# Reordering the first loads of a two-layer attention and gated-MLP kernel, with twelve idle matmuls ahead of them

## The chip, the cores and the metric

The kernel runs on one core of a Trainium2 chip. The metric is the time of one execution in device microseconds (us), from 1 core; several executions are timed and the median is quoted. A profile records one execution. Its span, from the first to the last instruction, is 1.8 us shorter than the time of the same execution (span 1628.9 belongs to 1630.68). Ratios are computed as the mean time of one kernel's runs over that of the other's of the same rounds, so they are not quite the ratio of the medians that are quoted.

## The reference, cut to what matters

```
x = x + A(layernorm(x))      # linear attention, D = 1024, 32 heads, S = 2048 rows
x = x + B(layernorm(x))      # gated MLP, F = 3584
x = x + A(layernorm(x))      # the same weights again
x = x + B(layernorm(x))
```

Only the beginning of the first A matters: normalise rows of x, transpose them, and multiply by the weights of k (`wqkv[:, D:2D]`). Weights and x are bf16, sums f32.

## The kernel before

S is worked on in blocks of 128 rows: x0, x1 and so on are such blocks (256 KB each in bf16). Weights come in tiles of 1 MB (`k0`, `k1`: the two halves of the k weights, 8 slices of 128 rows by 512 columns). The first four blocks go through a hand-ordered head:

```python
def head(self):
    H = self.KT // 2                        # 4: half of the 8 slices of a weight tile
    zero = self.ep.tile([P, NW], BF16, tag="e")
    nc.vector.memset(zero, 0.0)
    idle = self.ps3.tile([P, NW], F32, tag="b")
    for _ in range(10):                     # nothing uses them: they only keep PE working
        nc.tensor.matmul(idle, lhsT=zero[:, 0:P], rhs=zero, start=True, stop=True)

    k0, k1, v0, q0, q1 = (ring.place() for _ in range(5))
    self.load_x(0, 0, nc.scalar)            # first half of x0 on ACT's queue
    self.load_x(0, 1)                       # second half on SP's queue
    self.load_x(1, None, nc.scalar)
    k0(0, H)                                # weights are on SP's queue
    self.load_x(2, None, nc.scalar)
    k0(H, 2 * H)
    self.load_x(3, None, nc.scalar)
    k1()
    q0()
    self.load_x(4)
    ...                                     # x5 and later, q1, v0
```

```python
def block0():                               # head_units: order of DVE and ACT is as written
    stat(0, 0)                              # DVE: statistics of x0, first half
    stat(0, 1)
    rstd(0)                                 # DVE, then two ACTIVATEs
    stat(1, 0)                              # DVE: fills the wait for rstd, needs x1
    scale(0, 0)                             # DVE
    scale(0, 1)
    t0 = turn(0, 0)                         # PE: four transposes
    t1 = turn(0, 1)
    t0("s")                                 # ACT copies them to SBUF
    stat(1, 1)
    rstd(1)
    t1("v")                                 # DVE copies
    k(0, 0, between)                        # PE: 8 matmuls, x0 with k0; `between` turns x1
```

The fifth matmul of `k(0, 0)` is the first to need the second half of k0. The next eight are x1 with k0, the eight after that x0 with k1, and only then come the transposes of x2.

Of the kernel before, what the change touches and what calls it, by code (L numbers as in the profile page):

```python
# [18 lines left out]
class _Ring:  # L19
# [9 lines left out]
    def place(self):  # L29

        name, src = self.plan[self.loaded]
        t = self.pool.tile([P, 8, NW], BF16, tag="w")
        self.tiles[name] = t
        self.loaded += 1
        return lambda lo=0, hi=8: self.nc.sync.dma_start(out=t[:, lo:hi, :], in_=src[:, lo:hi, :])

    def load_to(self, n):
        while self.loaded < min(n, len(self.plan)):
# [40 lines left out]
class _Net:  # L79
# [131 lines left out]
    def head(self):  # L211

        nc, tc, ring = self.nc, self.tc, self.ring
        H = self.KT // 2

        zero = self.ep.tile([P, NW], BF16, tag="e")
        nc.vector.memset(zero, 0.0)
        idle = self.ps3.tile([P, NW], F32, tag="b")
        for _ in range(10):
            nc.tensor.matmul(idle, lhsT=zero[:, 0:P], rhs=zero, start=True, stop=True)  # L220

        k0, k1, v0, q0, q1 = (ring.place() for _ in range(5))
        self.load_x(0, 0, nc.scalar)
        self.load_x(0, 1)
        self.load_x(1, None, nc.scalar)
        k0(0, H)
        self.load_x(2, None, nc.scalar)
        k0(H, 2 * H)
        self.load_x(3, None, nc.scalar)
        k1()  # L230
        q0()
        self.load_x(4)
        self.load_x(5)
        self.load_x(6)
        self.load_x(7)
        q1()
        for t in range(8, self.ST):
            self.load_x(t)
        v0()
        src = self.xb  # L240
        self.xnT[0, 0] = self.xnTp.tile([P, self.KT, QT * P], BF16, tag="xnT", name="xnT0_0")
        stats = [self.small.tile([P, 2, nc.vector.BN_STATS_DIM], F32, tag="stats", name=f"st{j}")
                 for j in range(QT)]
        rs, xn = {}, {}

        def stat(j, c):
            self.ln_stat(j, src[j], c, stats[j])

        def rstd(j):
            rs[j] = self.ln_rstd(stats[j])  # L250
            xn[j] = self.xn_home(0, j)

        def scale(j, h=None):
            self.ln_scale(src[j], *rs[j], xn[j], h)

        def turn(j, h):
            tp = self.ps3.tile([P, H, P], BF16, tag="b")
            for i in range(H):
                kt = h * H + i
                nc.tensor.transpose(tp[:, i, :], xn[j][:, kt * P:(kt + 1) * P], self.ident)  # L260
            dst = self.xnT[0, 0][:, h * H:(h + 1) * H, j * P:(j + 1) * P]

            def take(engine):
                if engine == "v":
                    nc.vector.tensor_copy(out=dst, in_=tp)
                else:
                    nc.scalar.activation(out=dst, in_=tp, func=ACT.Copy)

            return take

        return stat, rstd, scale, turn
# [468 lines left out]
```

## Time and profile before

| | before |
|---|---|
| median time | 1629.3 us (1629.17 to 1629.80, 4 runs) |
| profiled execution | 1630.68 us, span 1628.9 us |
| PE busy | 1621.7 us of the span |
| wait of PE for the second half of k0 | 1.73 us |
| its load: issued, landed | 1.66, 10.19 us |

The list of DMA issues for the moment at which the second half of k0 (SP) and x2 (ACT) are issued; the columns are what is loaded, the issuing queue, count, size, and us from issue to landing:

```profile
t<-in_A_wqkv_dram SPq DMA_DIRECT2D x1, 512.0 KB, 8.5
x<-in_A_x_dram ACTq DMA_DIRECT2D x1, 256.0 KB, 7.7
```

Both are issued within 0.01 us and both take about 8 us, and x3 follows on ACT's queue: the three are moved at the same time.

### The profile page before, as it was taken

How to read it: one execution, taken by the hardware profiler on the slowest of the kernel's cores; microseconds unless marked ns; L12 is line 12 of the kernel's file. 1: busy time of each engine (PE TensorE's matmuls, PEld its weight loads, DVE VectorE, ACT ScalarE, POOL GpSimd, SP SyncE). 2: the span in 40 equal slices, each digit the busy share in tenths (PEclk: the TensorE clock that was granted, in tenths of full speed). 3: DMA queues.
4: the chain of work that ended last, by engine and by line, in shares of the span. 5: the costliest groups of instructions: out<-in, count | busy, mean ns of one | idle time of the engine just before them, and what ended most of it. 6: DMA issues, size and time to landing. Idle time of an engine off the chain costs nothing.

```text
span 1628.9 us, 18772 instructions
## 1 busy us (share of the span) xinstructions
PE 1621.7 (100%) x7754; PEld 739.3 (45%) x7754; DVE 566.7 (35%) x940; ACT 331.8 (20%) x638; POOL 201.9 (12%) x134
## 2 busy tenths in 40 slices
PE   8999999999999999999999999999999999999999
PEld 4444444444444444444444444444444444444444
DVE  7845695213212222212165547942022111111211
ACT  5741212101110110111066312121011101101110
POOL 2349220000000000000023592100000000000000
DMA  7312647448445444544560147464554454454452
GB/s 245 65 52 56 178 71 206 144 148 232 155 143 190 160 151 161 168 147 137 168 128 1 53 93 250 85 193 146 182 165 152 155 184 155 145 166 154 155 162 71
DMA packets 298246, 235.06 MB, mean 144 GB/s; under 512 B 101296, under 2 KB 294192, under 8 KB 298160
## 3 DMA queue, kind: packets, MB, share of 16 engines
q1 hardware_dynamic: 292832, 228.75, 47.7%
q10 hardware_dynamic: 5328, 5.11, 0.9%
q8 instruction: 60, 0.98, 0.3%
q14 instruction: 26, 0.21, 0.0%
HBM read 201.33 MB, written 8.39 MB: 129 GB/s over the span
## 4 chain that ended last, share of the span: by engine, by line
PE 98%; ACT 1%; DVE 1%; DMA 1%; issue 0%; SPq 0%; DVEq 0%
PE pu L639 24%; PE pg L639 24%; PE acc L663 23%; PE ps L404 12%; PE ps L530 7%; PE ps L439 7%; DMA t<-in_A_wqkv_dram 1%; PE kv L452 0%; PE acc_last L663 0%; ACT e L351 0%; ACT e L350 0%; PE fold L515 0%; DVE st L138 0%; ACT e L352 0%; DVE slab L358 0%
## 5 line engine op out<-in xcount | busy, mean ns | idle before, releaser
L639 PEld LDWEIGHTS <-t 128*128 128x128 bf16 x3584 | 350.3, 98 | 423.2
L639 PE MATMUL pu<-xnT,t 128*128 128x512 bf16 x1792 | 423.5, 379 | 0.0
L639 PE MATMUL pg<-xnT,t 128*128 128x512 bf16 x1792 | 423.4, 379 | 0.0
L663 PE MATMUL acc<-t,hT 128*128 128x512 bf16 x1764 | 382.5, 379 | 0.0
L645 DVE TENSOR_TENSOR hT<-pu,rg 128x512 bf16<-128x512 f32 x224 | 154.7, 691 | 572.0 <-PE pu L639 572.0
L644 ACT ACTIVATE rg<-pg 128x512 f32<-128x512 f32 x224 | 133.5, 596 | 737.3 <-PE pg L639 737.0
L663 PEld LDWEIGHTS <-hT 128*128 128x128 bf16 x1820 | 177.9, 98 | 209.1
L404 PE MATMUL ps<-t,xnT 128*128 128x512 bf16 x1024 | 224.3, 380 | 2.2 <-DMA t<-in_A_wqkv_dram 1.7
L404 PEld LDWEIGHTS <-xnT 128*128 128x128 bf16 x1024 | 99.2, 98 | 122.3 <-issue 4.3
L530 PE MATMUL ps<-T,pqT 128*128 128x512 bf16 x512 | 111.2, 379 | 0.0
L145 ACT ACTIVATE rstd<-mv,eps 128x1 f32<-128x1 f32 x64 | 18.7, 293 | 334.1 <-DVE mv L143 333.9
L680 DVE TENSOR_TENSOR xo<-x,acc 128x512 bf16<-128x512 f32 x31 | 21.3, 688 | 170.3 <-PE acc L663 170.3
L483 POOL TENSOR_TENSOR prod<-pq,zrow 128x1024 f32<-128x1024 bf16 x32 | 67.9, 2122 | 85.9 <-DVE den L488 72.5
L138 DVE BATCH_NORM_STATS2 stats<-x 128x6 f32<-128x512 f32 (+1 forms) x120 | 78.0, 673 | 0.8
L530 PEld LDWEIGHTS <-pqT 128*128 128x128 bf16 x512 | 49.9, 98 | 60.4 <-issue 0.5
L419 POOL CAST ksum<-x 128x512 f32<-128x512 bf16 x2 | 1.7, 866 | 605.4 <-DVE x L358 605.4
L677 DVE TENSOR_TENSOR x<-x,acc 128x512 f32<-128x512 f32 x32 | 21.6, 675 | 138.5 <-PE acc L663 137.4
L421 POOL TENSOR_TENSOR ksum<-ksum,slab 128x512 f32<-128x512 f32 x46 | 54.0, 1183 | 84.6 <-DVE slab L358 75.1
L358 DVE SCALAR_TENSOR_TENSOR pq<-ps,e 128x512 bf16<-128x512 f32 x64 | 44.0, 688 | 53.9 <-ACT e L352 52.2
L495 POOL TENSOR_TENSOR pq<-pq,den 128x1024 bf16<-128x1024 bf16 x32 | 61.7, 1933 | 3.1 <-DVE den L490 3.1
L488 DVE TENSOR_REDUCE den<-prod 128x32 f32<-128x1024 f32 x32 | 39.0, 1217 | 53.9 <-POOL prod L483 53.9
L439 PE MATMUL ps<-slab,x 128*128 128x512 bf16 x256 | 56.6, 379 | 0.0
(57 smaller groups left out, 596.0 us busy)
## 6 DMA issues: line engine op xcount, KB each, us to landing
t<-in_B_W_gate_dram SPq DMA_DIRECT2D x56, 1024.0 KB, 7.1
t<-in_B_W_up_dram SPq DMA_DIRECT2D x56, 1024.0 KB, 5.4
t<-in_B_W_down_dram SPq DMA_DIRECT2D x64, 896.0 KB, 5.2
t<-in_A_wqkv_dram SPq DMA_DIRECT2D x11, 1024.0 KB, 5.6
t<-in_A_wo_dram SPq DMA_DIRECT2D x4, 1024.0 KB, 7.2
away<-x SPq DMA_DIRECT2D x8, 512.0 KB, 4.4
x<-away SPq DMA_DIRECT2D x8, 512.0 KB, 8.5
out_dram<-xo ACTq DMA_DIRECT2D x31, 128.0 KB, 2.5
```

Source lines behind the costliest of these rows:

```text
L138: self.nc.vector.bn_stats(out=stats[:, c, :], in_=src[:, c * fmax:(c + 1) * fmax])
L358: nc.vector.scalar_tensor_tensor(out=out, in0=ps, scalar=0.0, in1=e, op0=ALU.max, op1=ALU.add)
L404: nc.tensor.matmul(by_row(ps), lhsT=self.xnT[l, l_q][:, kt, j * P:(j + 1) * P], rhs=w[:, kt, :].rearrange("p (b i d) -> p i b d", i=R, d=H ...
L421: nc.gpsimd.tensor_tensor(out=ksum[:, cols], in0=ksum[:, cols], in1=pk, op=ALU.add)
L439: nc.tensor.matmul(ps, lhsT=self.xn[l, t][:, d * P:(d + 1) * P], rhs=self.pk[l, t][:, h * NW:(h + 1) * NW], start=(t == 0), stop=(t == sel ...
L483: nc.gpsimd.tensor_tensor(out=prod, in0=pq_of[sc, j], in1=zrow, op=ALU.mult)
L495: nc.gpsimd.tensor_tensor(out=heads(pq), in0=heads(pq), in1=den[:, :].unsqueeze(2).to_broadcast([P, D // HD, HD]), op=ALU.mult)
L530: nc.tensor.matmul(ps, lhsT=pqT[sc][:, g, j * P:(j + 1) * P], rhs=T[g // 2][:, g % 2, n2 * NW:(n2 + 1) * NW], start=(g == 0), stop=(g == G ...
L639: nc.tensor.matmul(ps, lhsT=w[:, kt, fi * P:(fi + 1) * P], rhs=self.xnT[l, q][:, kt, :], start=(kt == 0), stop=(kt == KT - 1))
L644: nc.scalar.activation(out=rg, in_=pg, func=ACT.Relu)
L645: nc.vector.tensor_tensor(out=h[:, fi, :], in0=pu, in1=rg, op=ALU.mult)
L663: nc.tensor.matmul(ps[:, 0:n], lhsT=hT[ft // 4][:, ft % 4, j * P:(j + 1) * P], rhs=wd[:, k, i * n:(i + 1) * n], start=(ft == 0), stop=(ft ...
```

## The change

The first weights should meet less competition: x2 and x3 leave ACT's queue and line up behind k0 and behind k1 on SP's; the halves of x0 swap queues; PE gets two more idle matmuls to bridge the time until x0 is ready.

```diff
-        for _ in range(10):
+        for _ in range(12):
             nc.tensor.matmul(idle, lhsT=zero[:, 0:P], rhs=zero, start=True, stop=True)
...
-        self.load_x(0, 0, nc.scalar)
-        self.load_x(0, 1)
-        self.load_x(1, None, nc.scalar)
+        self.load_x(0, 0)
+        self.load_x(0, 1, nc.scalar)
         k0(0, H)
-        self.load_x(2, None, nc.scalar)
+        self.load_x(1, None, nc.scalar)
         k0(H, 2 * H)
-        self.load_x(3, None, nc.scalar)
+        self.load_x(2)
         k1()
+        self.load_x(3)
         q0()
```

(The load function also gets a `queue` argument that nothing uses.)

More of the change, by code (lines that the diff above doesn't have):

```diff
@@ L34, in place @@
         self.loaded += 1
-        return lambda lo=0, hi=8: self.nc.sync.dma_start(out=t[:, lo:hi, :], in_=src[:, lo:hi, :])
+        return lambda lo=0, hi=8, queue=None: (queue or self.nc.sync).dma_start(
+            out=t[:, lo:hi, :], in_=src[:, lo:hi, :])
     def load_to(self, n):
@@ L218, in head @@
         idle = self.ps3.tile([P, NW], F32, tag="b")
-        for _ in range(10):
+        for _ in range(12):
             nc.tensor.matmul(idle, lhsT=zero[:, 0:P], rhs=zero, start=True, stop=True)
         k0, k1, v0, q0, q1 = (ring.place() for _ in range(5))
-        self.load_x(0, 0, nc.scalar)
-        self.load_x(0, 1)
+        self.load_x(0, 0)
+        self.load_x(0, 1, nc.scalar)
+        k0(0, H)
         self.load_x(1, None, nc.scalar)
-        k0(0, H)
-        self.load_x(2, None, nc.scalar)
         k0(H, 2 * H)
-        self.load_x(3, None, nc.scalar)
+        self.load_x(2)
         k1()
+        self.load_x(3)
         q0()
```

## The prediction

> **What bounds the kernel now.** I read the page first, then the waits of PE, then the timeline of the first 20 us, since the diff touches nothing but the kernel's head. The page's first part and its chain of work:
>
> ```profile
> span 1628.9 us, 18772 instructions
> PE 1621.7 (100%) x7754; PEld 739.3 (45%) x7754; DVE 566.7 (35%) x940; ACT 331.8 (20%) x638; POOL 201.9 (12%) x134
> ...
> PE 98%; ACT 1%; DVE 1%; DMA 1%; issue 0%; SPq 0%; DVEq 0%
> ```
>
> PE is busy 1621.7 of 1628.9 us. All its idle time is 7.2 us, 0.44% of the span. A change that only moves loads can't win more than that, whatever it does. The waits of PE over the first 20 us say how much of the 7.2 us lies where the diff works:
>
> ```profile
> PE ps L404 <- DMA t<-in_A_wqkv_dram: 1.7, 1, 1.7
> PE idle L220 <- DVE zero L217: 1.3, 1, 1.3
> PE tp L260 <- DVE x L154: 0.6, 1, 0.6
> PE ps L404 <- ACT xnT L267: 0.4, 1, 0.4
> ```
>
> That is 4.0 us; nearly all of the rest is the tail after the last matmul. Three of the four are not a matter of weights: 1.3 us until the zero tile exists, 0.6 us until the first normalised x block, 0.4 us until its transposed copy. The 1.7 us is the wait for the second half of the first weight tile k0. The timeline shows the hole (the columns are start, duration, engine, line):
>
> ```profile
> 5.22 0.68 DVE L138 BATCH_NORM_STATS2 st<-x 128x6 f32<-128x512 bf16 x1
> ...
> 5.90 0.74 DVE L154 TENSOR_SCALAR x<-x,mv,rstd 128x512 bf16<-128x512 bf16 x2
> ...
> 7.46 1.04 PE L404 MATMUL ps<-t,xnT 128*128 128x512 bf16 x4 [0.37 <-ACT xnT L267]
> ...
> 8.08 0.73 DVE L154 TENSOR_SCALAR x<-x,mv,rstd 128x512 bf16<-128x512 bf16 x2 [0.31 <-ACT rstd L146]
> 10.23 0.59 PE L404 MATMUL ps<-t,xnT 128*128 128x512 bf16 x2 [1.73 <-DMA t<-in_A_wqkv_dram]
> ```
>
> Four matmuls run on the half of k0 that has landed, then PE stands from 8.50 to 10.23. When the loads land I worked out from the list of DMA issues, taken for short windows, as start plus time to landing: SP's x0 half 3.57, ACT's x0 half 3.75, x1 5.19, k0's first half 5.73, x2 9.34, **k0's second half 10.19**, x3 10.45, k1 13.37, q0 16.35. So the second half of k0, issued at 1.66, took 8.5 us for 512 KB: x2 and x3 (256 KB each) came from the other queue at the same time. The table of windows of 1 us shows that the engines were full then, not idle:
>
> ```profile
> 4.00:5.00 1.00, 1.00 (x4) 0.34 (x3) 1.00 (x2) 0.00 (x0) 0.00 (x0) 1.00 1.07 388
> 5.00:6.00 1.00, 0.79 (x2) 0.00 (x0) 0.97 (x4) 0.50 (x2) 0.00 (x0) 1.00 0.91 302
> 6.00:7.00 1.00, 0.62 (x8) 0.45 (x8) 1.00 (x3) 0.19 (x1) 0.00 (x0) 1.00 0.96 346
> 7.00:8.00 1.00, 0.63 (x5) 0.31 (x4) 0.74 (x3) 0.85 (x3) 0.00 (x0) 1.00 1.03 365
> 8.00:9.00 1.00, 0.50 (x3) 0.10 (x2) 0.73 (x2) 0.05 (x1) 0.00 (x0) 1.00 1.06 347
> ```
>
> The last three columns are clock, DMA share and GB/s. What counts in the head is therefore how many bytes go before k0, and then before k1.
>
> **What the Trainium skill says.** The page "DMA: Bandwidth & Descriptors", section "Queues, rings and completion order", says that SP and ACT each have one ring on each of the same 16 DMA engines, and that an engine takes turns between them packet by packet. Its section "Issuing engines are not separate DMA queues" adds that issuing from several engines only saves the sequencer's time. The trace agrees: the sum stays at 302 to 388 GB/s whether one queue or both have work. A second queue thus gives no bandwidth, but what is on it takes a share from the first. "TensorE: Matmul & The Clock Gate", Part 1, says that the array starts at half clock and is released after about 3.4 us of work, at a moment that varies between runs. The trace agrees: idle matmuls start 0.43 us apart up to the last at 5.16, the first projections from 7.46 on 0.216 us apart, and the 1.73 us hole does not bring the slow clock back.
>
> **The change part by part.**
>
> *The two halves of x0 swap queues.* The half on SP landed 0.18 us before that on ACT. The statistics of the first half start at 3.78 because ACT's half lands at 3.75; after the change they should start near 3.60. But VectorE works in program order: before it scales x0 it takes the first statistics of x1 (5.22 to 5.90), and x1 lands at 5.19. x1 keeps its place as second on ACT behind a half of x0, so it should land at 5.19 again, and the scaling still starts at 5.90. Gain: 0.
>
> *Two more idle matmuls.* The tenth starts at 5.16. At 0.427 us each the eleventh starts at 5.59, the twelfth at 6.01, and the first transpose can't start before 6.44; it now starts at 6.38, when x0 is scaled. Cost: 0.06 us if the clock is still slow, 0 if it is released earlier. They fill a 0.58 us wait of PE, so they could only help in a run in which that wait delays the release of the clock; this trace doesn't show such a delay.
>
> *x2 and x3 leave the ACT queue; x2 goes behind k0, x3 behind k1.* Sum of bytes ahead of each end, all queues, against the running sum of the table of windows (18 GB/s in 1 to 2 us, then 228, 385, 388, 302, 346, 365, 347, 369, 356, 346, which is 1.02 MB by 5 us, 1.32 by 6, 1.67 by 7, 2.03 by 8, 2.38 by 9, 2.75 by 10, 3.10 by 11):
> - k0 before: x0 to x3 and k0, 2.10 MB, moved by 8.2 us, landed at 10.19: 2.0 us after that. For its first half, 1.05 MB, moved by 5.1 and landed at 5.73, this lag was 0.6 us. For k1, 3.15 MB, moved by 11.1, landed 13.37: 2.25 us.
> - k0 after: x0, x1 and k0, 1.57 MB, moved by 6.7 us; with a lag of 0.6 to 2.0 us it lands at **7.3 to 8.7**.
> - PE wants it at 8.34 (7.46 and four matmuls of about 0.22). The next thing PE needs, the transposes of x1, can go after VectorE's scaling, which is done by 8.49 for its first half. So nothing new stops PE there, and from this point everything moves forward by up to 10.23 - 8.34 = **1.89 us**.
> - k1 after: x0 to x2, k0, k1, 2.88 MB, moved by 10.4, so landing at **11.0 to 12.6**. Before, PE began with k1 at 13.41, when it had just landed; moved by 1.89 it wants it at 11.5. Wait: 0 to 1.1 us. Middle of the two lags: 11.8, a wait of 0.3.
> - x2 is behind k0 by 0.26 MB, 0.7 us: 8.0 to 9.4. VectorE wants it at 12.08 - 1.89 = 10.2. No wait. x3 lands at 11.7 to 13.4, wanted at 14.98 - 1.89 = 13.1. A wait of at most 0.3, beside that for k1.
> - q0 has the same 4.2 MB ahead of it and itself as before, so 16.35 again; its first use moves from 24.95 to about 23. No wait. The blocks x4 and later keep their sum of bytes too, and are used from 21.8 on.
>
> *Afterwards.* From 26.8 to about 42 us the chain goes through ScalarE (three ACTIVATEs of 0.58, 0.63 and 0.72, together 1.93 us a unit, against 8 x 0.216 = 1.73 us of matmuls), but that row starts from PE's results, so it starts as much earlier. From 44 us PE is the chain. Nothing hangs on a fixed time, so what the head gains stays: I take 1.89 - 0.3 for k1 - 0.1 for the rest (idle matmuls 0.06, changed landings) = 1.5 us, and shade it to 1.4.
>
> **The rivals.**
> 1. *The wait moves to k1.* If the lag of 2 us stays (one of the 16 engines was late: counting the semaphore packets of SP's queue, most engines had ended k0 by 8.0, the last at 9.66), k0 lands at 8.7 to 9.2 and k1 at 12.6. Before, k1 came at 13.37, so the gain is 0.8 us: 1628.6. For it: k1 and q0 show the same lag of 2.2 us, also in time when SP alone loads. Against it: the lag arises between 5.3 and 9.7 us, just when both queues load, and x1 and the first half of k0 hadn't it.
> 2. *Everything hidden.* No lag: the whole 1.89 us comes, perhaps 0.1 to 0.2 more where PE waited for VectorE at 19.28: 1627.4.
> 3. *The first chain gets longer.* x1 or the ACT half of x0 lands later, or the twelve matmuls meet a slow clock: the whole program shifts back by as much. A load that slips 0.5 us would leave 0.9 us. Only a PE that goes cold in the first projections could eat it all: 1629.4 or a little more. Against it: those first 1,024 KB (x0, x1, half of k0) go out in the same order and sizes as before, but for the swapped halves.
> 4. *A bound that takes it back.* ScalarE's stretch to 44 us is where a gain could be swallowed. But it never gets ahead of PE's start there, so I give it little.
>
> **Range and chances.** Before, 1629.38 us (1629.17 to 1629.80). Less 1.4 is **1628.0**. Full gain gives 1627.4, the lag case 1628.6; the runs before differ by 0.6 us among themselves, and another chip may differ as much, so 8 times in 10 between 1627.1 and 1629.2. Two per cent would be 32.6 us, more than four times all idle time of PE, and a loss of that size has no source in two matmuls and reordered loads: within 2% has 0.99, the others 0.005 each.
>
> **What would show it.** Right: in the waits of PE the 1.7 us on the k0 weights is gone or under 0.4; k0's second half lands at 7.3 to 8.7; the first projection still starts at 7.46 to 7.55; x1 still lands near 5.2; k1 lands at 11.0 to 12.6 and any new PE wait is for it; PE busy time stays within 1 us of 1621.7 while the span falls. Wrong: k0 still after 9.5 (then bytes ahead were not the reason), a first transpose that moves by over 0.2 us, the statistics of x2 or x3 waiting for their loads and PE for them, or a gain at 20 us that is gone at 50.

## The result, and the profile after

| | before | after |
|---|---|---|
| median | 1629.30 us | 1629.16 us |
| range, 4 runs each | 1629.17 to 1629.80 | 1628.77 to 1629.68 |
| ratio | | 0.9999, 95% interval 0.9981 to 1.0016 |
| span of the profiled execution | 1628.9 us | 1627.0 us |

The medians differ by 0.14 us, the two profiled spans by 1.9 us. First the profile after. Its span and engines:

```profile
span 1627.0 us, 18776 instructions
PE 1621.9 (100%) x7756; PEld 740.3 (46%) x7756; DVE 566.7 (35%) x940; ACT 331.8 (20%) x638; POOL 201.9 (12%) x134
```

PE does the same work, so the 1.9 us are idle time. The waits of PE in the head (what waited, for what, us in total, times, longest):

```profile
PE idle L221 <- DVE zero L218: 1.3, 1, 1.3
PE ps L405 <- ACT xnT L268: 0.4, 1, 0.4
PE tp L261 <- DVE x L155: 0.2, 1, 0.2
```

The wait for the weights is gone, and the wait for the scaled x0 went from 0.6 to 0.2 because the idle matmuls last longer. The timeline (start, duration, engine, line) answers to the lines shown of before; lines are one higher in the changed file:

```profile
5.29 0.69 DVE L139 BATCH_NORM_STATS2 st<-x 128x6 f32<-128x512 bf16 x1 [0.30 <-DMA x<-in_A_x_dram]
...
5.90 0.72 DVE L155 TENSOR_SCALAR x<-x,mv,rstd 128x512 bf16<-128x512 bf16 x2
...
7.44 1.47 PE L405 MATMUL ps<-t,xnT 128*128 128x512 bf16 x6 [0.37 <-ACT xnT L268]
...
8.74 0.39 PE L261 MATMUL tp<-ident,x 128*128 128x128 bf16 x4
```

Six matmuls run where four ran before, and the transposes of x1 follow at once: at 8.74 in place of 10.66. The second half of k0 landed at 7.47 and k1 at 11.16; both were in time. From there on everything is 1.9 us earlier: the transposes of x3 start at 17.37 in place of 19.28, and the span is 1609.6 us longer than that in both traces.

So the profiles show just what was predicted, and the times show next to nothing of it.

### The profile page after: what moved, and what is told of

The parts are those of the page before. It is cut to its first block, busy times and chain, and to the rows that moved or that the text cites. A ratio compares the mean times of both kernels' runs of the same rounds, so it can differ in the third digit from the quotient of the medians.

```text
span 1627.0 us, 18776 instructions
## 1 busy us (share of the span) xinstructions
PE 1621.9 (100%) x7756; PEld 740.3 (46%) x7756; DVE 566.7 (35%) x940; ACT 331.8 (20%) x638; POOL 201.9 (12%) x134
## 4 chain that ended last, share of the span: by engine, by line
PE 98%; ACT 1%; DVE 1%; issue 0%; DMA 0%; DVEq 0%
PE pg L640 24%; PE pu L640 24%; PE acc L664 23%; PE ps L405 12%; PE ps L531 7%; PE ps L440 7%; PE kv L453 0%; PE acc_last L664 0%; ACT e L352 0%; DMA x<-in_A_x_dram 0%; ACT e L351 0%; PE fold L516 0%; DVE st L139 0%; ACT e L353 0%; DVE slab L359 0%
```

## The experiments

Three theories stood against each other. **S**, straggler: the profiled execution of before was an unlucky one, in which one DMA engine ran late. **F**, fixed: the hole of 1.73 us is in every execution, and the four times are noise. **C**, clock: executions differ in when the clock of PE is released, and this, not the loads, moves the time. Later a fourth was added, **N**: a new wait, for k1, eats a part of the gain.

The traces give one number that makes them comparable. In thirteen of fourteen, span less the start of x3's transposes is 1609.6 us, within 0.1 (more_ahead: 1609.96). What differs happens before x3's transposes; nothing is given back later. The table collects what the traces show (us; "clock" is the start of the full-clock record in the trace; a dash where PE did not wait; three traces have no such record, and there the spacing of matmuls says that the clock was released before the time given):

| trace | clock | first transposes | k0, second half landed | wait for k0 | wait for k1 | x3's transposes | span |
|---|---|---|---|---|---|---|---|
| before | by 6.38 | 6.38 | 10.19 | 1.73 | - | 19.28 | 1628.9 |
| before_again | 6.33 | 6.29 | 8.89 | 0.51 | - | 17.98 | 1627.6 |
| before_third | 10.55 | 6.63 | 9.05 | - | - | 19.14 | 1628.8 |
| after | 5.50 | 6.35 | 7.47 | - | - | 17.37 | 1627.0 |
| after_again | 6.71 | 6.44 | 8.35 | - | 0.32 | 17.71 | 1627.3 |
| after_third | 5.99 | 6.29 | 7.25 | - | - | 17.30 | 1626.9 |
| loads_only | 5.98 | 6.47 | 8.42 | - | 0.45 | 17.76 | 1627.4 |
| idle_only | 6.95 | 6.57 | 8.75 | - | - | 17.85 | 1627.5 |
| k1_halves | 6.24 | 6.73 | 7.78 | - | - | 17.74 | 1627.3 |
| k1_halves_again | by 5.2 | 6.64 | 7.37 | - | - | 17.66 | 1627.2 |
| k1_x1_halves | 7.31 | 6.44 | 8.70 | - | - | 18.72 | 1628.4 |
| more_ahead | 10.65 | 7.33 | 9.30 | - | - | 19.54 | 1629.5 |
| idle6 | 9.88 | 6.34 | 7.97 | - | - | 18.65 | 1628.3 |
| x1_first | by 5.5 | 6.50 | 9.12 | 0.41 | - | 18.22 | 1627.8 |

(Landings are issue plus time to landing. Starts that come less than 0.1 us after such a landing are not counted as waits. x1_first also waits 0.52 us for the first half of k0.)

### before_again: the kernel before, unchanged

> The kernel before, unchanged, for a second trace of it and more times. Known: in the profiled executions k0's second half landed at 10.19 us and left a hole of 1.73 us on PE (span 1628.9), but four timed executions of it had a median of 1629.3, where that profiled one took 1630.68. Theory S (straggler): one DMA engine was late by 2 us in the profiled execution by accident; in most executions k0's second half lands near 8.5 to 9.2, the hole is 0.2 to 0.8 us. Then this trace most likely shows a hole under 1.0 us and a span of 1627.3 to 1628.2. Theory F (fixed): the late engine and the 1.73 us hole belong to this order of loads and come in every execution; then the hole is 1.5 to 2.0 us again, and the median time of before is 1.5 us or more above that of the change. Theory C (clock): executions differ by when the clock is released; then the hole may be as in either case, but the first transposes or projections run at 0.43 us spacing in some executions.

Measured: 1630.05 us median of five (1629.13, 1629.41, 1630.05, 1630.63, 1630.65); nine more executions of the kernel before on the same chip, 1629.43 median, two of them at 1630.6. The timeline of its trace, at the fifth matmul and at x3's transposes:

```profile
7.38 1.04 PE L404 MATMUL ps<-t,xnT 128*128 128x512 bf16 x4 [0.37 <-ACT xnT L267]
8.93 0.59 PE L404 MATMUL ps<-t,xnT 128*128 128x512 bf16 x2 [0.51 <-DMA t<-in_A_wqkv_dram]
...
17.98 0.62 PE L260 MATMUL tp<-ident,x 128*128 128x128 bf16 x8
```

The same kernel has a hole of 0.51 us here, not 1.73: k0's second half landed at 8.89, not at 10.19. Theory F is dead. The packet records tell why: each load has 16 semaphore packets in the trace, as many as there are DMA engines, and I read them as one from each. For k0's second half fifteen of these lie between 7.55 and 7.96 us and the last at 8.35. In the first trace of before most lie at 7.7 to 8.2, but one came at 8.62 and the last at 9.66. So two of the 16 engines were late there, one of them by far, and the load landed 0.5 us after the last packet in both traces. (Below, "a late engine" means this: one engine, or a few, that end well after the rest.)

### after_again: the change, unchanged

> The changed kernel, unchanged. Its first trace had no wait for k0 (landed at 7.4) or k1 and a span of 1627.0, the best of its four timed executions (1627.0, 1627.4, 1627.4, 1627.9). Theory S: no hole in nearly every execution; time 0.2 to 0.9 us under before in the mean of five rounds, since before's hole is mostly small. Theory F: 1.5 to 1.9 us under before. Theory C: spans vary by 0.4 to 0.9 us among executions of this same kernel while loads never make PE wait; a trace with a span near 1627.5 would show slow idle matmuls, transposes or projections after 5.5 us.

Measured: 1629.11 us (1628.70 to 1629.35), 0.3 us below the median of before on this chip. The trace has no wait for k0, but this:

```profile
9.87 1.90 PE L405 MATMUL ps<-t,xnT 128*128 128x512 bf16 x8
12.09 0.59 PE L405 MATMUL ps<-t,xnT 128*128 128x512 bf16 x2 [0.32 <-DMA t<-in_A_wqkv_dram]
```

PE waits 0.32 us for k1, which landed at 12.04, as the prediction's first rival had it. Here three engines were late: their updates of the semaphore for k0's second half came at 7.82, 8.02 and 8.35 us, the other thirteen by 7.20, and for k1 at 11.51, 11.71 and 12.04, the others by 10.86. Theory C's detail shows too: the clock was released at 6.71, the twelve idle matmuls ran at 0.427 us spacing, and the first transposes began at 6.44 and not when x0 was scaled, about 0.1 us earlier.

### loads_only: the change with ten idle matmuls

```diff
-        for _ in range(12):
+        for _ in range(10):
```

> The change without its two idle matmuls: loads as after, ten idle matmuls. S and F: the same as after within 0.1 us, PE waiting about 0.6 us for the scaled x0 (5.79 to 6.38) instead of 0.2, first projection at 7.4 to 7.5. C: where the clock is released late, the longer wait delays the release, so the mean of five rounds is 0.2 us or more above after.

Measured: four executions of 1628.75 to 1629.19 and one of 1630.71; median 1628.99, mean 1629.29. The usual execution has the whole gain of the change without its idle matmuls, so the loads alone bring it. The mean is 0.25 us above that of after_again (1629.04), all from the one long execution, which was not traced. It looks as C expects, but one execution doesn't show it. The trace has a wait of 0.45 us for k1, and this too is a late engine: fifteen of them ended k1 by 10.96 us, the last at 12.10.

### idle_only: before with twelve idle matmuls

```diff
-        for _ in range(10):
+        for _ in range(12):
```

> The kernel before with twelve idle matmuls in place of ten, loads as before. S and F: the same as before within 0.15 us (the wait of 0.58 us becomes 0 to 0.2, the first projection stays at 7.4 to 7.55). C: 0.2 us or more below before in the mean, if the two matmuls bring the clock's release forward in some executions.

Measured: 1629.25, 1629.26, 1629.27, 1629.34 and 1630.32; median 1629.27, mean 1629.49. In the usual execution two idle matmuls bring about 0.16 us (median 1629.27 against 1629.43). The one long execution was not traced, so twelve idle matmuls don't exclude every cause of a long execution (a late engine would still make one).

### k1_halves and k1_halves_again: k1 in two loads

```diff
-        k1()
+        k1(0, H)
+        k1(H, 2 * H)
         self.load_x(3)
```

> The change, with k1's load issued as two halves of 512 KB behind x2, x3 after both. In two of three traces with the changed loads PE waited 0.32 and 0.45 us for k1, which landed at 12.04 and 12.10. Theory S+N (the late DMA engine is an accident, and a new wait on k1 takes a part of the gain): the first half lands near 10.5, before its use at 11.4 to 11.8, the second near 12.0, used 0.86 us later; the k1 wait is gone, and the median is 0.2 to 0.4 us under the change's 1629.1. Rival (k1's wait doesn't set the end, VectorE's chain to the scaled blocks x2 and x3 does): the wait goes, but PE waits as much longer before the transposes of x2 or x3, and the time stays within 0.1 us.

> The change with k1 in two halves, on the same chip as the change. If the wait on k1 is what eats the change's gain, the median is 0.2 to 0.4 us below the change's. If it was only a faster execution or another chip: within 0.1 us of it.

Measured: 1628.87 us in the first job (1628.64 to 1629.77; before 1629.68 there), 1628.92 in the second (1628.72 to 1629.34), beside the change's 1628.95 on the same chip. The first half of k1 landed at 10.00 and 9.56, well before its use, and no trace has a wait for k1. But the change itself had no such wait in its third trace either, and the medians side by side are equal within 0.03 us. The expected 0.2 to 0.4 us is refuted: theory N is right in some executions (0.32 and 0.45 us, both with a late engine) and doesn't set the median. It is also not a version that clearly beats the change.

### k1_x1_halves: x1 in two loads as well

```diff
-        self.load_x(1, None, nc.scalar)
+        self.load_x(1, 0, nc.scalar)
+        self.load_x(1, 1, nc.scalar)
```

> The same, with x1 also loaded as two halves on ACT's queue. VectorE takes the statistics of x1's first half before it scales x0, and that waits for x1 (landed 5.2 to 5.4, statistics 5.25 to 5.41, scaling 5.86 to 6.02). With halves the first lands near 4.6, its statistics run at 4.8 to 5.5, the scaling starts near 5.6 and the first transposes near 6.1. If the first chain sets the end: 0.2 to 0.4 us below k1_halves. If k0's second half (7.5 to 8.4) sets it: PE waits for k0 instead by as much, and the time is that of k1_halves within 0.1 us.

Measured: 1630.17 us (1629.51 to 1630.97), 1.2 us longer than k1_halves where a gain was hoped for. The list of issues for 1.66 to 1.70 us:

```profile
t<-in_A_wqkv_dram SPq DMA_DIRECT2D x1, 512.0 KB, 7.0
x<-in_A_x_dram ACTq DMA_DIRECT2D x1, 128.0 KB, 6.4
```

The first half of x1 landed at 5.18, not near the expected 4.6. The second half, only 128 KB, needed 6.4 us and held up VectorE, as the timeline shows:

```profile
8.07 0.69 DVE L139 BATCH_NORM_STATS2 st<-x 128x6 f32<-128x512 bf16 x1 [1.54 <-DMA x<-in_A_x_dram]
```

It is the third load on ACT's queue, issued just after the second half of k0 on SP's. In the kernel before, x2 stands at that very place and had the same fate: the packet records show nothing on ACT's queue between 5.0 and 5.5 us, when x1 was through and x2 had been issued 3 us earlier. So in the kernel before x2 did not run ahead of k0's second half; the two started together, after k0's first half, and shared the engines.

### more_ahead: 512 KB more on ACT's queue, in the kernel before

```diff
         self.load_x(3, None, nc.scalar)
+        self.load_x(4, None, nc.scalar)
+        self.load_x(5, None, nc.scalar)
         k1()
         q0()
-        self.load_x(4)
-        self.load_x(5)
```

> The kernel before with x4 and x5 also on ACT's queue, so 512 KB more before k0's second half. Theory B (bytes ahead of k0 set its landing, at 0.35 to 0.37 MB per us): it lands 1.4 us later than in the kernel before with no late engine (8.8), at 10.0 to 10.4; the hole on PE is 1.4 to 2.0 us, and the time 1.2 to 1.5 us above before. Rival (SP's queue gets a share that is independent of what waits on ACT's queue, and the late engine alone makes the hole): k0 lands as before, time within 0.3 us of before.

Measured: 1631.75 us (1630.94 to 1632.44), 2.1 us above before. The time came, but not by the expected way, so this experiment did not test what it was made for. k0's second half landed at 9.30, later than 8.89 or 9.05 but not at 10.0 to 10.4: most of x4 and x5 wasn't ahead of it. What cost time was that ScalarE's instruction stream stood at the second of the two issues. The timeline of ScalarE, and the row of that issue alone from a shorter stretch (5 to 8 us):

```profile
3.43 2.82 ACTq L369 DMA_DIRECT2D x<-in_A_x_dram  x2
...
5.92 0.34 ACTq L369 DMA_DIRECT2D x<-in_A_x_dram  x1
...
6.30 0.29 ACT L145 ACTIVATE rstd<-mv,eps 128x1 f32<-128x1 f32 x1 [4.28 <-DVE st L138]
```

The first row joins two issues, of x4 and x5, and what lies between them. Each took only about 0.34 us, but x5's began at 5.92: in the trace it waits for a semaphore that k0's first half had set when it landed at 5.89, and ScalarE's later instructions stood behind it. So its ACTIVATEs for x0 ran at 6.30 in place of 5.34, the first transposes came at 7.33, PE idled 1.54 us before them, and the clock was released only at 10.65. (x1 landed at 5.51 here, which by itself makes the first transposes late, as in before_third below, but there they came at 6.63.) The theory that bytes ahead set k0's landing is neither confirmed nor refuted by the time; the landing of 9.30 fits the view that only what the other queue moves while k0 moves counts, not all that is issued there.

### idle6: the change with six idle matmuls

```diff
-        for _ in range(12):
+        for _ in range(6):
```

> The changed loads with six idle matmuls in place of twelve: PE is idle from about 4.1 to 6.4 us. Theory C (a wait of PE in the head delays the release of the clock, which explains executions 1.2 us longer, of which the change with twelve had none in 9 and kernels with ten 6 in 24): most executions are 1 us or more above the change, the trace shows the release after 8 us and transposes 0.107 us apart, projections 0.427 apart. Without such an effect: time and trace as the change within 0.2 us.

Measured: 1630.01, 1630.02, 1630.05, 1630.20 and 1631.06; median 1630.05. (This was another chip than that of after_again; before had a median of 1629.68 on it, and k1_halves, the same loads but for k1 in two parts, 1628.87, so with six idle matmuls nothing is left of the change's gain.) The loads were in time, k0's second half at 7.97. The timeline:

```profile
6.34 1.03 PE L261 MATMUL tp<-ident,x 128*128 128x128 bf16 x8 [2.25 <-DVE x L155]
7.63 2.56 PE L405 MATMUL ps<-t,xnT 128*128 128x512 bf16 x6 [0.26 <-ACT xnT L268]
10.03 0.39 PE L261 MATMUL tp<-ident,x 128*128 128x128 bf16 x4
```

PE waited 2.25 us for x0. The first transposes start when they always do, but eight of them take 1.03 us where the change needed 0.72, and six matmuls take 2.56 where it needed 1.47: matmuls start 0.427 us apart and transposes 0.107. The clock was released at 9.88. x3's transposes start at 18.65, 1.3 us later than in the best traces of the change. So a wait of PE in the first microseconds, which by itself costs nothing, costs 1 us through the clock. Theory C's mechanism is shown. The clock records have one more sign of it: the full-clock record is 1621.33 us long in the eight traces with a release by 7.31 us, and 1617.92 in the three late ones (idle6, before_third, more_ahead). That is 3.41 us shorter in each, as if each late release had missed one step of 3.41 us. A wait that comes after the release did no such harm: k1_halves_again waited 0.87 us for x0 with the clock released by 5.2, and its transposes ran at full speed.

### before_third: the kernel before again

> The kernel before once more, for a third trace of it and for more executions. So far k0's second half landed at 10.19 and 8.89 us, holes of 1.73 and 0.51 us. Theory S+N (the first trace caught an execution with one DMA engine late by 1.9 us; usual is 0.3 to 0.6): hole 0.2 to 0.9 us, span 1627.4 to 1627.9, unless this execution is one of the longer ones (about one in three, 1.2 us more), when either the hole is over 1.2 us or the clock is released after 7.5 us. Theory F (fixed 1.73 us hole): 1.5 to 2.0 us.

Measured: 1629.89 us median of five, nine more of before on this chip 1629.87; 6 of these 14 above 1630.0. By luck the traced execution is one of the long ones, 1630.54:

```profile
6.63 1.03 PE L260 MATMUL tp<-ident,x 128*128 128x128 bf16 x8 [0.84 <-DVE x L154]
7.93 2.74 PE L404 MATMUL ps<-t,xnT 128*128 128x512 bf16 x6 [0.26 <-ACT xnT L267]
10.47 0.43 PE L260 MATMUL tp<-ident,x 128*128 128x128 bf16 x4
```

k0's second half landed at 9.05 and PE never waited for it, because the four matmuls before it ran at half speed until then. The ten idle matmuls end at 5.79; x1 landed at 5.54, its statistics held up the scaling of x0, and PE waited 0.84 us for that. The clock was released at 10.55. Set beside idle6 this is the same picture. Set beside before_again, whose wait was 0.50 us and whose clock came at 6.33, x3's transposes are 1.16 us later; at the first transposes it was 0.34 us (6.63 against 6.29), so most of it is the clock.

So a long execution of the kernel before has at least two causes: a late DMA engine (its first trace) and a late clock (this one).

### after_third: the change again

> The change once more, beside before on the same chip. Theory S+N: median 0.15 to 0.5 us below before, nearly all of its executions in one group; no wait for k0; a wait for k1 of 0 to 0.5 us by how late one DMA engine is. Theory F: 1.5 us or more below.

Measured: 1628.95 us (1628.74 to 1629.56), 0.92 us below before's 1629.87 on this chip (ratio 0.9995, 95% interval 0.9982 to 1.0007). No wait for k0 or k1:

```profile
7.37 1.47 PE L405 MATMUL ps<-t,xnT 128*128 128x512 bf16 x6 [0.37 <-ACT xnT L268]
...
17.30 0.62 PE L261 MATMUL tp<-ident,x 128*128 128x128 bf16 x8
```

The gain is more than the 0.15 to 0.5 us expected of the median, since on this chip six of fourteen executions of before were long ones.

### x1_first: x1 on SP's queue ahead of k0, k1 in halves

```diff
-        k0(0, H)
-        self.load_x(1, None, nc.scalar)
+        self.load_x(1)
+        k0(0, H)
```

> k1 in two halves and x1 as one load on SP's queue ahead of k0, so ACT's queue has only half of x0. x1 should land at 4.2 to 4.5 in place of 5.2 to 5.6, with k0's first half as before near 5.8 (the same bytes before it). Then the statistics of x1's first half fit into VectorE's wait for the scale, the scaling starts at 5.5 to 5.7 in place of 5.86 to 6.3 and the first projection at 7.0 to 7.3. If the first chain sets the end: 0.2 to 0.5 us below k1_halves. If k0's second half does (7.5 to 8.4, wanted at 8.0): PE waits for it and the time is that of k1_halves. If the clock does (transposes now earlier than its release in many executions): no gain or a longer time, with transposes 0.107 us apart.

Measured: 1629.07 us (1628.86 to 1629.67); no gain over 1628.92. x1 landed earlier, at 4.66, but the halves of x0 landed at 3.87 and 4.06 in place of about 3.5 and 3.65, and both halves of k0 late, at 7.69 and 9.12. PE waited for both:

```profile
7.73 1.02 PE L406 MATMUL ps<-t,xnT 128*128 128x512 bf16 x4 [0.52 <-DMA t<-in_A_wqkv_dram]
9.16 0.59 PE L406 MATMUL ps<-t,xnT 128*128 128x512 bf16 x2 [0.41 <-DMA t<-in_A_wqkv_dram]
```

The table of windows has the reason, as far as a trace can give one (last column GB/s):

```profile
4.00:5.00 1.00, 1.00 (x4) 0.34 (x3) 1.00 (x2) 0.00 (x0) 0.00 (x0) 1.00 0.58 194
5.00:6.00 1.00, 1.00 (x4) 0.25 (x2) 0.95 (x3) 0.50 (x2) 0.00 (x0) 1.00 0.77 249
```

With nearly everything on SP's queue the engines moved 194 and 249 GB/s here, where the trace of before had 388 and 302 in the same two windows. (The third number from the end, the clock, reads 1.00 in these tables although the idle matmuls start 0.427 us apart at that time, so it doesn't show the slow start.) It is not simply that one queue is slow: in the trace of after SP's queue is alone from 5 us on, and the same table has 358 and 377 GB/s for 5 to 7 us. Why this order is slow is open; one trace shows it.

## Why the prediction was right or wrong

The measured median, 1629.16 us, lies within 1627.1 to 1629.2, but only by 0.04 us, 1.2 us above the forecast of 1628.0: that is the width of the range and luck. The class, within 2%, was right, as it could hardly fail to be. The forecast gain of 1.4 us was not what the comparison showed (0.14), nor what more executions show. Taking the three jobs in which before and the change ran together: before has a mean of 1629.77 in 32 executions, the change 1629.07 in 14, so **0.7 us**, half of the forecast (0.20, 0.73 and 0.88 in the three; from the spread of the times I estimate a standard error of 0.13). No single job shows it: the 95% interval of each ratio includes 1. By its steps:

- **The ceiling** from PE's idle time: right, and the reason why the class was safe.
- **The halves of x0**: right, gain 0. The statistics started at 3.46 in place of 3.78, the scaling of x0 at 5.90 in both, since VectorE's statistics of x1 come between.
- **k0 lands at 7.3 to 8.7**: right within 0.05 us; 7.47, 8.35 and 7.25 in the three traces. The reason, fewer bytes ahead, fits: with the loads of before it landed at 8.75 to 9.05 in the three traces without a very late engine (before_again, before_third, idle_only), in after and after_third at 7.25 to 7.47. That is about 1.5 us, as 0.52 MB less at 0.35 MB per us gives (an estimate from the prediction's table of windows). No experiment tested the bytes alone.
- **1.89 us forward**: right for the two traces it compares (10.23 to 8.31 for the fifth matmul, 1.92 us) and wrong as a forecast. This is the step that was mis-sized. PE wants the load at about 8.3, so of the 1.5 us by which it comes earlier only what lies after 8.3 can be gained. The prediction took the 1.73 us hole of one profiled execution for what the kernel before does. The hole is 0.51 us in a second trace and absent in a third, where a late clock hides it. Between those traces that have neither a late engine nor a late clock, before_again and after_third, x3's transposes go from 17.98 to 17.30: **0.68 us**. The warning was in the material: the profiled execution took 1630.68 us, the timed ones 1629.17 to 1629.80.
- **The first rival**, that the wait moves to k1: true in two of five traces with these loads and k1 as one load, 0.32 and 0.45 us (the forecast took 0.3), so a part of the gain is given back in some executions. k1_halves removed it and the median didn't move, so it is not what limits the typical execution.
- **The late engine** as part of that rival: the prediction counted the semaphore packets and saw a late engine (it names one; x2 and k1 had four late ones each in that trace), but treated it as a thing that stays or goes with the order of loads. It comes and goes between executions of the same kernel: the last packet of k0's second half came at 9.66 and at 8.35 us.
- **Two idle matmuls**: the cost, 0.06 us with a slow clock, was about right (0.1 in after_again). That they gain nothing is about right for the usual execution (0.16 us in idle_only) and doubtful for the others. The prediction named the case in which they would help and left it out because the one trace did not show it. In the third trace of before it shows, with x3's transposes 1.16 us late, and six idle matmuls made all five executions long (idle6). That twelve in place of ten prevent it is not shown.
- **Nothing is given back later**: right; span less the start of x3's transposes is 1609.6 us in all traces of before and after.

How the 0.7 us divides is partly argued, not shown. In the same 32 executions of before, 11 lie above 1630.0 (mean 1630.45; one more of nine on the chip where the change did not run), the other 21 have a mean of 1629.42. The change has none of 14 above 1630.0 (nor has k1_halves any of 10). The usual execution thus gains 1629.42 - 1629.07 = 0.35 us, from the loads: loads_only, without the idle matmuls, has 1628.94 as the mean of its four usual executions. The rest, (11 x 1630.45 + 21 x 1629.42) / 32 - 1629.42 = 0.35 us, is the long executions that are no more. Which of them were late clocks, which late engines, is known for one of them (before_third) and for the first profiled execution, which is not among the 32. The changed loads take the late engines' long executions away by themselves, as far as two traces show: late engines cost waits of 0.32 and 0.45 us there (after_again, loads_only), and neither execution was long. That twelve idle matmuls prevent late clocks is shown as a mechanism by idle6 and before_third, and is likely, not proved, as the reason for none in 14, since loads_only had one long execution of five and idle_only one of five as well.

Still open: what makes one or a few DMA engines late in some executions, and why x1 lands anywhere from 5.2 to 5.6 us in traces of the same order of loads, which now sets the start of the first transposes (6.29 to 6.73 us). No version clearly better than the change was found.

## What to carry to other kernels

A profile is one execution: before sizing a wait by it, compare its time with the timed runs of the same kernel, and where it is not in their midst, take a second trace. In a head of a few microseconds, keep PE working until the data is there, a little longer than the traced execution needs, because there, before the clock is released, a wait of 0.84 us cost about a microsecond (before_third). Loads that share the engines with an urgent one should be issued behind it, and not third in line on the other queue.

## What the Trainium skill lacked or had wrong

- "TensorE: Matmul & The Clock Gate", Part 1, says the clock is released after one busy window of about 3.4 us, but not how much idle time a window may hold. Here a wait of 0.50 us between idle matmuls and transposes still let it come at 6.33 us (before_again), and one of 0.84 us went with a release at 10.55 (before_third). If windows are 3.4 us, the one that ended near 7.1 held that wait; this is an estimate from the page's figure, and the clock records fit it (1621.33 us long, or 1617.92 in the three late traces, 3.41 apart). The page's remark that the ramp costs under 1% of a kernel agrees: about 1.2 of 1629 us.
- "DMA: Bandwidth & Descriptors", section "Latency and other measured facts", says that engines 7 and 15 are usually slower, with a cause that it limits to another way of issuing. It doesn't say that one to four engines of 16 can lag by 0.5 to 1.8 us in one execution and not in the next, on loads from SP and ACT (k1 in loads_only: fifteen by 10.96 us, the last at 12.10; in after all by 11.16). The packed trace doesn't tell which engines they are.
- The same page, section "Issuing engines are not separate DMA queues", says that issuing from several engines only saves the sequencer's time. In x1_first, with almost all on one queue, the rate between 3 and 6 us was 194 to 249 GB/s against 302 to 388 with two queues in before (but 358 with one in after, from 5 to 6 us), so what the second queue is worth there is open.
- No section of that page gives the delay of a load issued on one queue while the other queue's earlier loads are unfinished: 128 KB as third load on ACT's queue took 6.4 us (k1_x1_halves), and nothing moved on ACT's queue between 5.0 and 5.5 us though x2 had been issued at 1.67 (before).
